# Fetching the rows of every block in quarters of 64 columns and turning them on VectorE

## The chip, the cores and the metric

The kernel runs on one core of a Trainium2 chip. The metric is the device time of one execution in microseconds, as the median of several runs. Where the profile is read, "the span" is the time from the first to the last instruction of one profiled execution.

## The reference: a Fourier mixing, then a mixture of experts

```python
# x: (8, 2496, 256) float32
X = np.fft.fft(x, axis=1)
X = np.fft.fft(X, axis=2)
x = X.real.astype(np.float32).reshape(19968, 256)
logits = x @ w_gate                                # 8 experts
expert_idx = np.argmax(logits, axis=1)
probs = np.exp(logits - logits.max(-1, keepdims=True))
probs /= probs.sum(-1, keepdims=True) + 1e-09
gate_w = probs[np.arange(N), expert_idx]
...
for e in range(E):                                 # rows sorted by expert
    h = np.maximum(x_sorted[lo:hi] @ w1[e], 0.0)   # 256 -> 1024
    y_sorted[lo:hi] = h @ w2[e]                    # 1024 -> 256
return gate_w[:, None] * y_sorted[inv_perm]
```

Each of 19968 rows goes to the one of eight experts that the gate chooses. All data are float32.

## The kernel before

**Two kinds of work are woven into each other.** For each of eight batches the Fourier part (`first`, `regroup`, `second`) computes the batch's 2496 rows, chooses an expert for each (`route`) and scatters the rows, each with its row number and its gate weight behind it (258 floats), to a table `Xs` in DRAM, in which each expert has its own region. The scatter is a series of indirect DMAs on GpSimd's queue (`send`). After a batch, VectorE works out how many full blocks of rows of one expert there are (`plan`), and the expert part (`experts`) works through such blocks. The two parts are generators, and the emission order of the program, which is also each engine's order, follows from how the main loop steps them.

**Blocks.** `rounds` fixes the list of blocks ahead of time: after batch 0 two blocks of 256 rows and four of 128, after batch 1 four of 256, after batch 2 three of 512, after each later batch five of 512, and at the end seven of 256 and 21 of 128 rows, of which a count made at run time says how many are real (`needed`: TensorE branches around the products of the others). These are 66 blocks. `halved(b, size)` is true for the blocks of 512 rows after batch 3 and later and for the seven of 256 rows at the end, 32 blocks; it is false for the other 34 (25 of 128 rows, six of 256, three of 512). Halved blocks compute their first product with seven half-size products in place of eight (`seven`, which needs sums of parts of w1, made by `Left`, and of the rows, made by `right`); the blocks for which `quartered` is true do so with the second product too (`lower`).

**A block's steps.** `fetch_rows` (SyncE's queue) reads the block's rows from `Xs` into one of three buffers `xb`; `fetch_weights` (SyncE's queue, after it) reads w1 and w2 of its expert, 1 MB each, into one of three buffers each. Both are called up to two blocks ahead, and a buffer is free when the block three before is done with it; with `xb` that is its last use of the gate weights, the scaling of `y` on ScalarE (L849 or L674). `turn` brings the rows to the form that the first product needs, columns on the partitions: `xT`[p, c, r] is column 2p + c of row r, with the odd columns' sign changed. There is one buffer `xT`, so a block's turn comes after the first products of the block before. Then TensorE computes `ph` = w1 times `xT` (L222), VectorE (L808) and ScalarE (L810) bring it through the ReLU to `hT`, TensorE computes `py` = `hT` times w2, ScalarE scales it to `y` by the gate weight in `meta` (L849), and GpSimd scatters `y` to the output by the row numbers `ro` (L237; `ro` is made from `meta` at L767). The turn of block k + 1 is stepped between the products `py` of block k, or, where block k is quartered, inside `lower` behind its first, third and fifth product.

**The two ways to turn.** Where `halved` is true, `fetch_rows` reads the rows in four DMAs, one for each quarter of 64 columns (L538): quarter q goes to partitions 32q to 32q + 31, so that row 32j + k of the block lies on partition 32q + k at position j. A fifth DMA (L542) reads the row numbers and gate weights, 8 bytes of each row. VectorE's transpose of 32x32 pieces (L587) then makes `xT` for 256 rows at once, and ScalarE changes the odd columns' sign in place (L589). Where `halved` is false, one DMA (L533) reads whole rows, n = size / 128 neighbouring rows to a partition. TensorE transposes each 128x128 piece, even columns and odd columns, with an identity matrix (L595) to the PSUM tile `pt`, and VectorE multiplies it by +1 and -1 (`alt`) on its way to `xT` (L596).

A DMA on SyncE's queue waits in order, both for its buffer and for the transfer that last used its semaphore.

Of the kernel before, what the change touches and what calls it, by code (L numbers as in the profile page):

```python
# [12 lines left out]
F32 = mybir.dt.float32  # L13
BF16 = mybir.dt.bfloat16
I32 = mybir.dt.int32
ALU = mybir.AluOpType
ACTF = mybir.ActivationFunctionType
# [3 lines left out]
B, S, D = 8, 2496, 256  # L21
# [16 lines left out]
BIG, BLK, REST = 512, 256, 128  # L38
# [8 lines left out]
def free(ap, offset, *dims):  # L47
    return bass.AP(ap.tensor, ap.offset + offset, [list(ap.ap[0])] + [list(d) for d in dims])


def bc(ap, axis, n):
    shape = list(ap.shape)
    shape.insert(axis, n)
    return ap[tuple([slice(None)] * axis + [None])].to_broadcast(shape)


def shape_consts():

    c = {}
    n1 = np.arange(NA)[:, None]  # L60
    r = np.arange(NP)
    k1 = r // 2
    im = r % 2

    def wave(n2, f):
        return f(2 * np.pi / S * ((NB * n1 + n2) * k1 % S))

    w1 = [np.where(im, wave(n2, np.sin), wave(n2, np.cos)) for n2 in range(1, NS)]
    for f in (np.cos, np.sin):
        w1 += [np.where(im, 0.0, wave(0, f)), np.where(im, wave(NS, f), 0.0)]  # L70
    c["w1"] = np.stack(w1, 1) * (k1 < NK)

    u, cs, s = np.meshgrid(np.arange(NU), np.arange(2), np.arange(NS), indexing="ij")
    u, cs, s = (v.reshape(-1, 1) for v in (u, cs, s))
    k2 = np.arange(NB)
    t = 2 * np.pi / NB * ((s + 1) * k2 % NB)
    end = np.where(cs, 1.0 - 2.0 * (k2 % 2), 1.0)
    even = np.where(s == NS - 1, end, np.where(cs, -np.sin(t), np.cos(t)))
    odd = np.where(s == NS - 1, end, np.where(cs, np.cos(t), np.sin(t)))
    own = (u == np.arange(NU)).astype(float)  # L80
    c["m2"] = np.stack([(own[:, :, None] * m[:, None, :]).reshape(GP, GP) for m in (even, odd)], 1)

    rot = np.zeros((GP, GP))
    for p in range(GP):
        if p % NS == NS - 1:
            rot[p, p] = 1.0
        elif p // NS % 2:
            rot[p, p - NS] = -1.0
        else:
            rot[p, p + NS] = 1.0  # L90
    c["rot"] = rot

    d = np.arange(H)[:, None]
    m = np.arange(D + 1)
    t = 2 * np.pi / D * (d * m % D)
    rc, rs = np.cos(t), -np.sin(t)
    rs[0] = 1.0 - 2.0 * (m % 2)
    full = np.concatenate([rc[:, :D], rs[:, :D]], 0)


    rd = np.zeros((H, 2, 2 * E + NY + 1))
    sign = 1.0 - 2.0 * (m[:NY] % 2)
    rd[:, 0, 0:NY] = sign * rc[:, 0:NY]
    rs[0] = 0.0
    rd[0, 1, 2 * E] = 1.0
    rd[:, 1, 2 * E + 1:] = sign * rs[:, 0:NY]
    c["rd"] = rd
    c["alt"] = np.broadcast_to(np.array([1.0, -1.0]), (128, 2))
    c["rt"] = full.T.reshape(2, 128, D).transpose(1, 0, 2)

    p = np.arange(128)[:, None, None, None]
    h = np.arange(2)[None, :, None, None]
    g = np.arange(HW)[None, None, :, None]
    mir = np.arange(2)
    tau = 128 * (HW * h + g) + p
    k1 = tau // NB
    k = k1 + NA * (tau % NB)
    bad = (k1 >= NK) | ((mir == 1) & ((k1 == 0) | (k1 == NK - 1)))
    row = np.where(bad, 0, np.where(mir, S - k, k))
    c["row"] = row.reshape(128, 2, NSL)  # L120
    c["good"] = 1.0 - bad.reshape(128, 2, NSL)
    c["far"] = OUT * bad.reshape(128, 2, NSL)
    c["rev"] = np.broadcast_to(E - np.arange(E), (128, E))
    c["cap"] = np.broadcast_to(CAP * np.arange(E), (128, E))
    c["sgn"] = np.where(np.arange(128) == 0, 1.0, -1.0)[:, None]
    c["lane"] = np.arange(128)[:, None]
    c["tri"] = np.triu(np.ones((128, 128)), 1)
    c["ident"] = np.eye(128)
    return {n: np.ascontiguousarray(v, dtype=np.float32) for n, v in c.items()}


# [60 lines left out]
def halved(b, size):  # L192

    return size == 512 and b > 2 or size == 256 and b == B - 1
# [22 lines left out]
def kernel(ctx: ExitStack, tc, x, w_gate, w1, w2, out):  # L217
    nc = tc.nc
    vec, act, pool = nc.vector, nc.scalar, nc.gpsimd
# [5 lines left out]
    Xs = nc.dram_tensor("Xs", (ROWS, W), F32, kind="Internal").ap()  # L225

    def const_dram(name, v):
        return nc.inline_tensor(v, name=f"c_{name}").ap()
# [17 lines left out]
    def taken(ins, b):  # L246
        ins = getattr(ins, "ins", ins)
        if b + 1 < B:
            tc.declare_no_dep(ins, group=f"xs{b + 1}", reason="a block has rows of its round's batches alone")
        tc.add_to_no_dep_group("taken", ins)  # L250
# [7 lines left out]
    pse = ctx.enter_context(tc.tile_pool(name="pse", bufs=1, space=PSUM))  # L258
# [4 lines left out]

    ctx.enter_context(tc.manual_schedule())
    consts = shape_consts()

    side = [n for n in consts if n not in ("w1", "rt")]
    packed = np.zeros((128, sum(consts[n][0].size for n in side)), np.float32)
    table = cp.tile(list(packed.shape), F32, name="table")
    con, k = {}, 0  # L270
# [9 lines left out]
    wg = cp.tile([128, 2, E], F32, name="wg")  # L280
    tri = cp.tile([128, 128], BF16, name="tri16")
    ones = cp.tile([128, 128], BF16, name="ones16")
    ident = con["ident"]
    waves = const_dram("w1", consts["w1"])

    def load(b, q):
# [239 lines left out]
    def fetch_rows(b, size, tab, i):  # L526


        n = size // 128
        row = nc.sync.value_load(tab[:, 0, i:i + 1], min_val=0, max_val=ROWS - size)  # L530
        xb = bp.tile([128, BIG // 128, W], F32, tag="xb", name="xb", bufs=3)
        if not halved(b, size):
            taken(nc.sync.dma_start(out=xb[:, 0:n].rearrange("p t c -> p (t c)"),  # L533
                                    in_=Xs[ds(row, size)].rearrange("(p t) c -> p (t c)", t=n)), b)
            return xb, xb[:, 0:n, D:]
        flat = xb[:].rearrange("p t c -> p (t c)")
        for q in range(4):
            taken(nc.sync.dma_start(  # L538
                out=flat[32 * q:32 * q + 32, 0:2 * size].rearrange("p (j e) -> p j e", e=64),
                in_=Xs[ds(row, size), 64 * q:64 * q + 64].rearrange("(j k) e -> k j e", k=32)), b)  # L540
        meta = flat[:, 4 * D:4 * D + 2 * n].rearrange("p (t c) -> p t c", c=2)
        taken(nc.sync.dma_start(out=meta, in_=Xs[ds(row, size), D:].rearrange("(t p) c -> p t c", p=128)), b)  # L542
        return flat, meta
# [27 lines left out]
    def right(xs, b11, b12, b21, b22, eng=vec):  # L571

        o = [xs[:, k] for k in range(3)]
        eng.tensor_tensor(o[0], b12, b11, op=sub)
        eng.tensor_tensor(o[1], b22, o[0], op=sub)
        eng.tensor_tensor(o[2], b21, o[1], op=sub)
        eng.tensor_tensor(b12, b22, b12, op=sub)
        return b11, b21, b22, o[2], o[0], o[1], b12

    def turn(b, size, xb):  # L580


        xT = bp.tile([128, 2, BIG], F32, tag="xT", name="xT", bufs=1)
        n = min(size // 128, 2)
        for h in range(-(-size // 256)):
            if halved(b, size):
                vec.transpose(free(xT[:], 256 * h, [32, 8], [BIG, 2], [1, 32]),  # L587
                              free(xb, 512 * h, [64, 8], [1, 2], [2, 32]))
                act.activation(xT[:, 1, 256 * h:256 * h + 256], xT[:, 1, 256 * h:256 * h + 256], ACTF.Copy, scale=-1.0)  # L589
                yield xT  # L590
                continue
            pt = pse.tile([128, 2, n, 128], F32, tag="e", name="pt")
            for c in range(2):
                for t in range(n):
                    nc.tensor.transpose(pt[:, c, t], xb[:, 2 * h + t, c:D:2], ident[:])  # L595
            vec.tensor_tensor(xT[:, :, 256 * h:256 * h + 128 * n], pt[:].rearrange("p c t k -> p c (t k)"),  # L596
                              bc(con["alt"][:], 2, 128 * n), op=ALU.mult)
            yield xT
        if halved(b, size):
            th = size // 2  # L600
            xs = bp.tile([128, 3, th], F32, tag="xs", name="xs", bufs=1)
            r = right(xs, *(xT[:, c, k * th:(k + 1) * th] for c in range(2) for k in range(2)))
            yield r
# [109 lines left out]
    def experts(todo):  # L713
# [35 lines left out]
        for k, (b, size, last, at) in enumerate(todo):  # L749
            n, m = size // 128, BIG // size  # L750
            if not k:
                while todo[0][:3] not in tabs:
                    yield 0, False
                fetch_some(0, 1)
                while b not in whole:
                    yield 0, True
                fetch_some(0)
                for _ in range(9):
                    yield 0, False
                for xT in turn(b, size, xbs[0][0]):  # L760
                    pass
# [163 lines left out]
    for _ in first(0):  # L925
# [8 lines left out]
        out=Xs[E * CAP:].rearrange("(k p) w -> p k w", k=BLK // 128), in_=bc(pad[:], 1, BLK // 128)), "xs"), 0)  # L934
# [100 lines left out]
```

## Time and profile before

| | |
|---|---|
| median of 3 runs | 1286.0 us (1285.17 to 1287.41) |
| the profiled execution's own time | 1297.33 us |
| its span | 1295.5 us |
| mean granted TensorE clock | 0.971 |
| DMA packets of the span | 134023, 249.75 MB, mean 193 GB/s; 85065 of them under 512 B |
| row fetches: whole rows (L533), quarters (L538), their 8-byte parts (L542) | 34, 128, 32 DMAs |

The stages of the span, by the windows view: the time of each stretch, TensorE's matmul and weight-load time, and the share of the 16 DMA engines.

| stretch, us | what runs | PE busy | PEld busy | DMA share | GB/s |
|---|---|---|---|---|---|
| 80 to 142 | rounds 0, batch 1 | 49.2 of 62 | 42.5 | 0.83 | 290 |
| 142 to 245 | rounds 0 and 1, batch 2 | 97.1 of 103 | 86.0 | 0.71 | 245 |
| 245 to 340 | round 2, batch 3 | 94.9 of 95 | 66.5 | 0.49 | 167 |
| 1070 to 1283 | blocks of 256 and 128 rows | 213.0 of 213 | 205.2 | 0.75 | 277 |
| 1283 to 1296 | the last blocks, not real, and the drain | 4.1 of 13 | 1.3 | 0.62 | 228 |

In the profile PE is a matmul on TensorE and PEld the loading of its weights, DVE is VectorE, ACT ScalarE, POOL GpSimd, and SPq the queue of SyncE, which issues most DMAs. A line of a timeline gives the start and the length in us, engine, source line, operation, the tile written and the tiles read, the shapes and a count; in brackets stands how long the engine had been idle and what ended that. "issue" means that it waited for nothing that the profile shows, "remote" and "another core or an unknown queue" that the profile can't name the releaser. L222 is the line of the helper through which all products go, so these are told apart by their tiles.

### The profile page before, as it was taken

Reading aid. Unit: us, or ns where it says so; the run is one execution under the profiler, and the core shown is the slowest. Engines: PE = TensorE matmul, PEld = TensorE weight load, DVE = VectorE, ACT = ScalarE, POOL = GpSimd, SP = SyncE. Lnnn points to the kernel's source line nnn. Section 1 sums busy time; section 2 is a strip of 40 time slices with the busy share of each in tenths; the row PEclk is TensorE's granted clock in tenths of the full one; section 3 lists DMA queues with packets and bytes.
Section 4 is the critical chain, followed back from the end, with each engine's and each line's share of the span. In section 5 each row is a group of like instructions: output and inputs, shape, how many; then the busy total and the mean of one; then the engine's idle time right before and its main releaser. Section 6 shows DMA issues by size and latency. Waiting matters only on the chain.

```text
span 1295.5 us, 20735 instructions
## 1 busy us (share of the span) xinstructions
PE 1237.7 (96%) x7003; PEld 1090.5 (84%) x7003; DVE 700.5 (54%) x1772; ACT 423.4 (33%) x1059; POOL 360.6 (28%) x355
## 2 busy tenths in 40 slices
PE   6769899899999999999999999999999999999997
PEld 4658788687688888888888888888889999999996
DVE  4554145244256655566356655467488774444662
ACT  1423133132244333443234333343333332222222
POOL 0244304314411531135111531145364221111112
PEclk6869999999999999999999999999999999999998
DMA  8877857726636853456433744344355237777776
GB/s 240 275 237 270 310 205 254 276 84 201 201 114 176 277 152 110 141 150 242 120 102 127 241 128 149 98 135 146 107 151 164 90 113 288 276 265 273 290 294 241
DMA packets 134023, 249.75 MB, mean 193 GB/s; under 512 B 85065, under 2 KB 99891, under 8 KB 114332
## 3 DMA queue, kind: packets, MB, share of 16 engines
q1 hardware_dynamic: 117143, 203.33, 48.3%
q0 software_dynamic: 15888, 42.14, 9.0%
q10 hardware_dynamic: 885, 2.94, 0.7%
q8 instruction: 57, 0.93, 0.3%
q14 instruction: 50, 0.41, 0.1%
HBM read 194.97 MB, written 54.83 MB: 193 GB/s over the span
## 4 chain that ended last, share of the span: by engine, by line
PE 70%; issue 18%; DMA 4%; POOL 3%; DVE 2%; another core or an unknown queue 2%; ACT 1%; SPq 0%; POOLq 0%; ACTq 0%; DVEq 0%
PE py L222 28%; PE a L222 7%; PE c L222 7%; PE ph L222 6%; PE p L222 5%; PE d L222 4%; PE b L222 4%; PE s L222 3%; PE e L222 3%; POOL out_dram L237 3%; DMA xq<-in_x_dram 2%; PE pt L595 1%; DMA Xs<-rows,pi 1%; DMA xb<-Xs 0%
## 5 line engine op out<-in xcount | busy, mean ns | idle before, releaser
L222 PE MATMUL py<-w_sb,hT 128*128 128x256 f32 x2016 | 455.9, 381 | 6.5 <-DVE hT L808 3.9
L222 PEld LDWEIGHTS py<-w_sb,hT 128*128 128x128 f32 x2016 | 379.5, 191 | 57.2 <-DVE hT L808 4.3
L237 POOL DMA_INDIRECT out_dram<-y,ro x163 | 160.8, 986 | 729.2 <-ACT y L849 497.9
L237 POOL DMA_INDIRECT Xs<-rows,pi x160 | 163.3, 1020 | 198.3 <-ACT pi L469 103.6
L222 PE MATMUL ph<-xT,w_sb 128*128 128x128 f32 (+2 forms) x992 | 172.4, 329 | 8.5 <-DVE hT L808 6.7
L222 PEld LDWEIGHTS ph<-xT,w_sb 128*128 128x128 f32 x992 | 136.1, 193 | 34.1 <-issue 17.2
L849 ACT ACTIVATE y<-py,xb 128x256 f32<-128x256 f32 x129 | 61.0, 473 | 313.5 <-PE py L222 271.6
L222 PE MATMUL a<-xT,w_sb 128*128 128x256 f32 (+1 forms) x512 | 117.5, 356 | 0.0
L808 DVE TENSOR_SCALAR hT<-ph 128x512 f32<-128x512 f32 x43 | 29.7, 691 | 161.9 <-issue 79.7
L633 DVE TENSOR_TENSOR u<-p,b 128x512 f32<-128x512 f32 x57 | 39.2, 687 | 132.9 <-PE b L222 96.7
L222 PEld LDWEIGHTS a<-xT,w_sb 128*128 128x128 f32 x512 | 89.2, 190 | 10.3 <-issue 0.2
L643 ACT ACTIVATE hT<-a 128x512 f32<-128x512 f32 x57 | 34.0, 597 | 151.2 <-PE a L222 133.6
L410 DVE COPY lg<-p 128x16 f32<-128x16 f32 x80 | 13.9, 174 | 121.0 <-ACT zs L407 117.5
L222 PE MATMUL s<-xq,w 104*112 104x256 f32 (+2 forms) x208 | 62.9, 427 | 11.1 <-DVE xq L299 10.9
L810 ACT ACTIVATE hT<-ph 128x512 f32<-128x512 f32 x55 | 32.8, 597 | 98.2 <-PE ph L222 71.0
L222 PEld LDWEIGHTS p<-table,t 120*128 120x128 f32 x352 | 54.3, 204 | 12.3 <-issue 6.6
L222 PE MATMUL p<-table,t 120*128 120x120 f32 (+1 forms) x352 | 58.2, 290 | 3.8 <-issue 2.7
L222 PE MATMUL c<-xT,ws 128*128 128x256 f32 (+1 forms) x256 | 59.1, 358 | 2.3 <-issue 1.7
L222 PE MATMUL p<-table,zz 128*128 128x145 f32 (+1 forms) x320 | 56.8, 302 | 3.8 <-issue 2.0
L222 PE MATMUL d<-xT,w_sb 128*128 128x256 f32 (+1 forms) x256 | 58.8, 357 | 0.0
L222 PE MATMUL e<-xs,w_sb 128*128 128x256 f32 (+1 forms) x256 | 58.7, 356 | 0.0
L222 PE MATMUL b<-xs,ws 128*128 128x256 f32 (+1 forms) x256 | 58.7, 356 | 0.0
(148 smaller groups left out, 1739.1 us busy)
## 6 DMA issues: line engine op xcount, KB each, us to landing
w_sb<-in_moe_w_dram SPq DMA_DIRECT2D x132, 1024.0 KB
xq<-in_x_dram SPq DMA_DIRECT2D x24, 896.0 KB
xb<-Xs SPq DMA_DIRECT2D x100, 128.0 KB
Td<-t SPq DMA_DIRECT2D x18, 448.0 KB
t<-Td SPq DMA_DIRECT2D x8, 768.0 KB
t<-Td SPq DMA_DIRECT2D x8, 640.0 KB
xb<-Xs SPq DMA_DIRECT2D x25, 129.0 KB
Td<-t ACTq DMA_DIRECT2D x6, 448.0 KB
```

Of the source, the lines that this page charges most:

```text
L222: nc.tensor.matmul(o, lhsT=lhsT, rhs=rhs, start=start, stop=stop, **kw)
L237: return unordered(pool.indirect_dma_start(out=dst, out_offset=bass.IndirectOffsetOnAxis(ap=idx, axis=0), in_=rows, in_offset=None, bounds ...
L410: vec.tensor_copy(lg[:, k:k + 2], p3[:, NY:NY + 2 * E].rearrange("p (m e) -> p m e", m=2))
L595: nc.tensor.transpose(pt[:, c, t], xb[:, 2 * h + t, c:D:2], ident[:])
L633: vec.tensor_tensor(u2[:], p1[:], b[:], op=add)
L643: act.activation(h11, a[:], ACTF.Relu)
L808: vec.tensor_scalar(o, ph[:], 0.0, None, op0=ALU.max)
L810: act.activation(o, ph[:], ACTF.Relu)
L849: act.activation(y[:], py[:], ACTF.Copy, scale=meta[:, i, 1:2])
```

## The change

The branch for whole rows goes out of `fetch_rows`, and the branch with TensorE's transposes out of `turn`. All 66 blocks are fetched in quarters and turned by VectorE, blocks of 128 rows in one piece of 128. The constants `alt` and `ident` go out of the table of constants. `halved` still decides how the products are computed.

```diff
@@ shape_consts
-    c["alt"] = np.broadcast_to(np.array([1.0, -1.0]), (128, 2))
...
-    c["ident"] = np.eye(128)
@@ fetch_rows
         xb = bp.tile([128, BIG // 128, W], F32, tag="xb", name="xb", bufs=3)
-        if not halved(b, size):
-            taken(nc.sync.dma_start(out=xb[:, 0:n].rearrange("p t c -> p (t c)"),
-                                    in_=Xs[ds(row, size)].rearrange("(p t) c -> p (t c)", t=n)), b)
-            return xb, xb[:, 0:n, D:]
         flat = xb[:].rearrange("p t c -> p (t c)")
         for q in range(4):
@@ turn
-        n = min(size // 128, 2)
+        n = min(size, 256)
         for h in range(-(-size // 256)):
-            if halved(b, size):
-                vec.transpose(free(xT[:], 256 * h, [32, 8], [BIG, 2], [1, 32]),
-                              free(xb, 512 * h, [64, 8], [1, 2], [2, 32]))
-                act.activation(xT[:, 1, 256 * h:256 * h + 256], xT[:, 1, 256 * h:256 * h + 256], ACTF.Copy, scale=-1.0)
-                yield xT
-                continue
-            pt = pse.tile([128, 2, n, 128], F32, tag="e", name="pt")
-            for c in range(2):
-                for t in range(n):
-                    nc.tensor.transpose(pt[:, c, t], xb[:, 2 * h + t, c:D:2], ident[:])
-            vec.tensor_tensor(xT[:, :, 256 * h:256 * h + 128 * n], pt[:].rearrange("p c t k -> p c (t k)"),
-                              bc(con["alt"][:], 2, 128 * n), op=ALU.mult)
+            vec.transpose(free(xT[:], 256 * h, [32, n // 32], [BIG, 2], [1, 32]),
+                          free(xb, 512 * h, [64, n // 32], [1, 2], [2, 32]))
+            odd = xT[:, 1, 256 * h:256 * h + n]
+            act.activation(odd, odd, ACTF.Copy, scale=-1.0)
             yield xT
```

More of the change, by code (lines that the diff above doesn't have):

```diff
@@ L282 @@
     ones = cp.tile([128, 128], BF16, name="ones16")
-    ident = con["ident"]
     waves = const_dram("w1", consts["w1"])
```

## The prediction, made before the changed kernel was run

> **What bounds the kernel now.** I read the page's busy shares first, then the slices, then the waits of the touched tiles, then the timeline of each stage that the change touches.
>
> ```profile
> PE 1237.7 (96%) x7003; PEld 1090.5 (84%) x7003; DVE 700.5 (54%) x1772; ACT 423.4 (33%) x1059; POOL 360.6 (28%) x355
> ...
> DMA  8877857726636853456433744344355237777776
> ```
>
> TensorE is busy 96% of the span and carries the chain of waits (the page gives it 70%, and most of the 18% "issue" is time between its own instructions). Each slice is 32.4 us. The DMA row is high at both ends, and there the touched blocks run: the 13 blocks of rounds 0 to 2 (83 to 340 us, slices 3 to 11) and the 21 last blocks of 128 rows (from 1070 us). The 25 blocks of 512 rows between them, and seven of 256 in the last stage, already work in the new way. The answers for the tiles `pt` and `xT` show what the change takes away and what takes its place:
>
> ```profile
> L595 PE MATMUL pt<-table,xb x98: 273/282/488, 86.0 to 1287.9; 128*128 128x128 f32 x98
> L596 DVE TENSOR_TENSOR xT<-pt,table x37: 405/418/692, 87.2 to 1288.4; 128x256 f32<-128x256 f32 x25, 128x512 f32<-128x512 f32 x12
> ```
>
> ```profile
> L587 DVE STREAM_TRANSPOSE xT<-xb x57: 668/704/711, 346.0 to 1253.4; 128x512 f32<-128x512 f32 x57
> L589 ACT ACTIVATE xT<-xT x57: 407/417/419, 346.8 to 1254.2; 128x256 f32<-128x256 f32 x57
> ```
>
> The numbers are ns, shortest/median/longest. In the touched blocks are 98 transposes on TensorE and 37 copies out of PSUM; the lines of L587 and L589 are the turn and the sign change that will take their place.
>
> **Removed: 98 transposes.** Their duration is not their price, because records of TensorE overlap. The timeline of one 128-row block, in the last stage:
>
> ```profile
> 1149.03 0.40 PE L595 MATMUL pt<-table,xb 128*128 128x128 f32 x2
> ...
> 1149.23 0.69 DVE L808 TENSOR_SCALAR hT<-ph 128x512 f32<-128x512 f32 x1 [3.22 <-PE ph L222]
> 1149.26 3.62 PE L222 MATMUL py<-w_sb,hT 128*128 128x256 f32 x16
> 1149.84 0.41 DVE L596 TENSOR_TENSOR xT<-pt,table 128x256 f32<-128x256 f32 x1
> ...
> 1152.50 0.19 PEld L222 LDWEIGHTS ph<-xT,w_sb 128*128 128x128 f32 x1
> ```
>
> From the first transpose's start to the next product's start is 1149.26 - 1149.03 = 0.23 us for two, so 0.115 us each. At 163.68 to 164.15 it is 0.47 for four. The Trainium skill ("TensorE: Matmul & The Clock Gate", Part 4) gives about 275 ns for a transpose in a kernel's context. The record's 282 ns agrees, but it is a latency: by that figure the change would free 98 x 0.275 = 27 us, by the spacing 98 x 0.115 = 11.3 us. I take the spacing. It is the most that can be gained from TensorE's own time.
>
> What of it counts:
> - The 21 last blocks: TensorE is busy 213.0 of 213 us from 1070 to 1283 us, so it is worth its full price there. Of the 42 transposes the last 6 are in the drain after 1283 us, where TensorE mostly waits: 36 x 0.115 = 4.1 us.
> - Rounds 0 to 2: 56 transposes. The first 4 stand behind a wait (below). The next 10 (to 142 us) run ahead of a TensorE stall that ends at 142.2 us (3.9 us for VectorE's hT, then "remote"), while the DMA engines are full; a stall that ends with a transfer swallows what was gained before it: 0. The next 18 (145 to 233 us, 2.1 us) run ahead of a like stall, 3.8 us at 239.9; I count half, 1.0. The last 24 (2.8 us) meet full TensorE until 340 us, but the round after begins with a wait for scattered rows at 336 to 341 us, which the last 8 feed: 16 x 0.115 = 1.8.
> Sum of gains: 4.1 + 1.0 + 1.8 = 6.9 us.
>
> **Added on VectorE and ScalarE.** A turn of 256 rows takes 0.70 us on VectorE where the copy took 0.68 to 0.69. For 128 rows no row stands there: below, half of it, 0.35; above, the whole, 0.70. VectorE's other operations go from 0.69 (512 wide) to 0.42 (256 wide), so I take 0.42, as now. The sign change is new on ScalarE: 12 x 0.42 + 25 x 0.28 (the 128x128 copies of L681 take 0.25) = 12 us in all, on an engine that is 33% busy. What hides both is the second half of the block: in the lines above VectorE finishes hT at 1149.92, would turn until 1150.34 and ScalarE negate until about 1150.65; TensorE needs xT at 1152.50 - 0.23. That is 1.6 us of margin; without it each block would lose the excess. A 128-row block after a 256-row one is turned inside `lower`: there the negation comes after the copy of `p1` in ScalarE's order, so the product that waits for this copy is not held. 0 us.
>
> **Moved: the wait for the rows.** Now TensorE itself waits for xb; then VectorE will, and behind it ScalarE's negation and the y copies. Where rows are early that is nothing. Where they are late, it is the first block of all, on the chain:
>
> ```profile
> 83.36 1.47 SPq L533 DMA_DIRECT2D xb<-Xs  x2
> ...
> 85.99 1.13 PE L595 MATMUL pt<-table,xb 128*128 128x128 f32 x4 [4.50 <-DMA xb<-Xs]
> ...
> 87.90 3.39 PE L222 MATMUL ph<-xT,w_sb 128*128 128x256 f32 x8 [0.78 <-DVE xT L596]
> ```
>
> and the nearest row for what replaces it, the first two fetches of the round at 340 us:
>
> ```profile
> 340.79 1.99 SPq L538 DMA_DIRECT2D xb<-Xs  x4
> 343.29 0.40 SPq L542 DMA_DIRECT2D xb<-Xs  x1
> ...
> 345.98 1.30 DVE L587 STREAM_TRANSPOSE xT<-xb 128x512 f32<-128x512 f32 x2 [5.84 <-DMA xb<-Xs]
> ```
>
> One transfer and a transpose took 87.90 - 83.36 = 4.54 us to the first product. A fetch of 512 rows in quarters took 345.98 - 340.79 = 5.19 us to VectorE's start. For 256 rows the packet records of the fetch at 1242.25 end 3.55 us after its first issue; with the semaphore I take 4.3, then 0.70 turn, and the odd half 0.47 later. First product at 88.4 and the second at 88.85: **+1.0 us**, and the 4 transposes there save nothing. The next start of a round, at 238.80, has 12 us until its xT is needed (251.2): 0. In the drain the last fetch (1283.56) lands about as late as now, but TensorE no longer waits for it (2.8 us at 1287.65): 0 to -0.5, taken as 0.
>
> **Added: 136 DMA issues on SyncE.** 34 fetches become 170 transfers. SyncE spends 343.69 - 340.79 = 2.9 us on a quartered fetch, 0.34 on a whole one. Behind it in SyncE's order stand the next block's w1 and w2, so these start 2.2 to 2.5 us later; in rounds 0 to 2 stores of Td and loads of x also stand there. In the last stage a 128-row block's weights are requested at 1147.86 and used at 1159.8, and 2 MB take 5.5 us: 4 us remain. The tight request is another: w1 of a 256-row block, for which VectorE waits (28.8 us over 6 waits at L569), after which the turned rows are ready 0.8 to 2.0 us before TensorE asks. That fetch is in quarters already, so SyncE doesn't delay it, and the saved transposes take only 0.23 us from the margin: 0.
>
> **Added: small packets.** The Trainium skill ("DMA: Bandwidth & Descriptors", Specifications; also "Rules for kernel authors") speaks against this: transfers under 512 B don't reach line rate. The trace's packet records say how much: 256 B take 21 ns, 8 B 10 ns, 1032 B 58 ns, on one of 16 engines. A 128-row block goes from 128 x 58 = 7.4 to 512 x 21 + 128 x 10 = 12.1 engine-us, +0.3 us. Read as half rate, the rule would make 132 KB at the stage's 277 GB/s 0.5 us longer. If DMA bounded the last stage, 21 blocks would lose 6 us by the trace and 10 by the rule, more than the gain; but its share there is 0.75 and becomes about 0.78, so I take 0. Between 122 and 142 us the engines are full, and two or three fetches there move the end of that stall: about +0.6 us at 0.2 to 0.3 each; bounds 0 and 2.
>
> **Sum** in the profiled execution: -6.9 + 1.0 + 0.6 = -5.3 us; with the drain's half and the +-1 of the stalls I say -6. Span 1295.5 becomes 1289.5, its own time 1297.3 becomes 1291.3. The profiled execution is 11.3 us over the median 1286.0; the difference carries over: **1280 us**.
>
> **The rivals.**
> 1. *All of it counts*: the stalls at 142 and 240 us are not tied to transfers, and shift or shrink. Gain 10 to 11.3, and up to 4.7 more (0.9 + 3.8) if the stall at 240 goes: about 1273. For it: the stalls are put down to "remote" and "issue", not to a DMA. Against: both end as the DMA engines drain. Chance 0.13.
> 2. *Nothing*: rounds 0 to 2 lose 3 to 4 us (longer fetches, full DMA) against 4.1 in the last stage: 1286. For it: DMA share 0.83 from 80 to 142 us. Chance 0.17.
> 3. *Slower*: late weights. Each small fetch holds SyncE 2.2 us longer ahead of w1 and w2, and the small packets lengthen what is in flight. If the DMA engines have no slack in rounds 0 and 1, the 8 blocks fetched from 88 to 191 us pay up to 2.2 us each, 17.6 at most; I take 9. If in the last stage w1 of the 256-row blocks comes late by over about 1 us (its margin), 6 blocks pay the rest, about 0.8 us each, 5 us. Together 14 against the gain of 6.9: 1293. It decides from the point where a fetch plus weights take longer than the block before them (7.2 us). For it: both stages are the DMA's fullest. Against: the order of the tight request, above, and 0.75 share. Chance 0.25.
> That the rows aren't turned rightly is none: the new layout puts row 128t+p at partition p in meta and in xT alike.
>
> **Numbers.** My forecast has 0.45, with a range of its own of 1276 to 1284. No change is within 0.2%, 2.6 us. Faster: 0.45 less its upper edge, and rival 1: 0.57; same 0.17; slower 0.26. Leaving out a tenth at each end: 1272 to 1293.
>
> **What would show it.** Right: no `pt`; 7.0 us instead of 7.25 from one 128-row block's first product to the next; first product of the first block near 88.8; the L569 waits near 29 us. Wrong: TensorE idle after 1070 us behind xT or w_sb; waits before 250 us that grew; SyncE's issues (over 1 us each) ahead of w_sb; stalls at 142 and 240 us moved by several us, which the sum can't foresee.

## The result, and the profile after

The changed kernel takes **1277.5 us** (median of 6 runs, 1275.2 to 1280.6) against 1286.8 (1285.2 to 1287.9, 6 runs beside it): a ratio of 0.9929, 95% interval 0.9913 to 0.9944, or 9.3 us less. The forecast was 1280.

The profiled execution of after has a span of 1273.3 us and its own time is 1275.2. That is 22 us less than before's profiled execution, and more than twice what the medians differ by: before's execution was itself 10.5 us above this median. Which part of these 22 us belongs to the change is the main question below. The page of after, rows as before:

```profile
PE 1220.9 (96%) x6905; PEld 1076.5 (85%) x6905; DVE 700.5 (55%) x1772; ACT 434.8 (34%) x1096; POOL 359.7 (28%) x355
...
DMA  8859988736745743584532843344453238778787
...
DMA packets 163210, 249.71 MB, mean 196 GB/s; under 512 B 118601, under 2 KB 130227, under 8 KB 143516
```

The 98 transposes are gone (7003 matmuls became 6905), VectorE's total has not moved (700.5 before and after), ScalarE has 11.4 us more, and there are 29,000 more packets (33,500 more under 512 B, and fewer of the larger ones that whole rows made). In the last stage (slices 33 to 39 of the DMA row) the engines are busier by a little, 0.80 from 1049 to 1240 us against 0.75 before (1070 to 1283 us). The answer for the tile `xT` gives the new turn, and the timeline the first block (start, length, then as before):

```profile
L579 DVE STREAM_TRANSPOSE xT<-xb x94: 433/699/712, 86.9 to 1267.0; 128x512 f32<-128x512 f32 x69, 128x256 f32<-128x256 f32 x25
L582 ACT ACTIVATE xT<-xT x94: 309/416/418, 87.7 to 1267.6; 128x256 f32<-128x256 f32 x69, 128x128 f32<-128x128 f32 x25
```

```profile
83.00 1.92 SPq L531 DMA_DIRECT2D xb<-Xs  x4
...
86.93 0.71 DVE L579 STREAM_TRANSPOSE xT<-xb 128x512 f32<-128x512 f32 x1 [7.27 <-DMA xb<-Xs]
...
87.70 3.50 PE L220 MATMUL ph<-xT,w_sb 128*128 128x256 f32 x8 [9.12 <-DVE ro L752]
```

The shortest turn, of 128 rows, is 0.43 us (0.42 was taken), the shortest negation 0.31 (0.28). The first product starts 4.70 us after its fetch was issued, against 4.54 before and 5.0 in the prediction.

To see where time came from, I set the last write of chosen blocks against each other in each trace. The 66 blocks are numbered from 0. Stretch A ends with block 11, the second block of 512 rows; C is the last stage, blocks 38 to 62, without its last three blocks; D are those three. Ratios are to the kernel before on the same chip. The pair `before` and `after` is the one of the result above; the four rows from `before_again` to `after_dummy` ran on a chip on which before took 1302.0 us, the four from `after_again` to `early_dummy` on one with 1287.0, the last four on one with 1285.2. One of the twelve runs of `tail_only`, of 1623.4 us at a granted clock of 0.742, is left out of its ratio.

| kernel | ratio (95%) | profiled, own us | A | C | D |
|---|---|---|---|---|---|
| before | 1 | 1297.3 | 328.8 | 216.8 | 6.9 |
| after | 0.9929 (0.9913 to 0.9944) | 1275.2 | 309.6 | 214.4 | 9.6 |
| before_again | one run, 1310.0 us | 1310.0 | 339.4 | 217.0 | 5.9 |
| early_only | 0.9962 (0.9940 to 0.9984) | 1297.3 | 328.7 | 217.1 | 7.4 |
| tail_only | 1.0011 (0.9994 to 1.0029) | 1304.2 | 334.3 | 214.2 | 9.3 |
| after_dummy | 1.0024 (1.0005 to 1.0043) | 1299.2 | 326.3 | 218.7 | 9.2 |
| after_again | 0.9927 (0.9907 to 0.9948) | 1279.7 | 312.4 | 215.8 | 9.4 |
| hybrid | 0.9912 (0.9891 to 0.9933) | 1276.3 | 309.3 | 216.4 | 6.9 |
| weights_first | 0.9910 (0.9890 to 0.9930) | 1272.4 | 306.9 | 212.0 | 11.9 |
| early_dummy | 0.9946 (0.9927 to 0.9965) | 1278.4 | 312.3 | 216.0 | 6.0 |
| early_only_2 | 0.9934 (0.9915 to 0.9953) | 1275.3 | 308.8 | 216.7 | 6.5 |
| early_dummy_2 | 0.9958 (0.9942 to 0.9974) | 1281.0 | 313.5 | 216.0 | 8.2 |
| issues_only | 1.0033 (1.0018 to 1.0047) | 1288.1 | 318.6 | 217.0 | 8.4 |
| best | 0.9895 (0.9877 to 0.9912) | 1272.9 | 311.2 | 212.2 | 5.6 |

Two stretches are left out: the one between A and C, which lies between 736.2 and 740.7 us in all of them, and the one from the last write's start to the end of the span, 3.5 to 5.9 us. Each row is one execution, and executions of one kernel can differ by several us in A (`before` and `before_again`, by 10.6, though on different chips), so the ratios decide and the stretches only say where to look. Already here the picture differs from the prediction's. The last stage, which was to bring most of the gain, is 1.0 to 2.4 us shorter in two traces of the same changed kernel and gives 2.5 to 2.7 us back in D; the gain is in A. Of the 19.2 us between before and after in A, 10.2 lie between before and `issues_only`, whose early rounds are the same.

### The profile page after: what moved, and what is told of

It reads as the page before. It is cut to its first block, busy times and chain, and to the rows that moved or that the text cites. A ratio compares the mean times of both kernels' runs of the same rounds, so it can differ in the third digit from the quotient of the medians.

```text
span 1273.3 us, 21052 instructions
## 1 busy us (share of the span) xinstructions
PE 1220.9 (96%) x6905; PEld 1076.5 (85%) x6905; DVE 700.5 (55%) x1772; ACT 434.8 (34%) x1096; POOL 359.7 (28%) x355
## 2 busy tenths in 40 slices
DMA packets 163210, 249.71 MB, mean 196 GB/s; under 512 B 118601, under 2 KB 130227, under 8 KB 143516
## 4 chain that ended last, share of the span: by engine, by line
PE 86%; DVE 5%; DMA 5%; issue 2%; ACT 1%; SPq 1%; POOL 0%; POOLq 0%; DVEq 0%; ACTq 0%
PE py L220 33%; PE ph L220 11%; PE c L220 10%; PE a L220 9%; PE d L220 6%; PE p L220 6%; PE b L220 5%; PE e L220 4%; PE s L220 3%; DMA w_sb<-in_moe_w_dram 2%; DMA xq<-in_x_dram 1%; DMA Td<-t 1%; SPq L531 0%; DMA xb<-Xs 0%; DVE xq L305 0%
## 5 line engine op out<-in xcount | busy, mean ns | idle before, releaser
L582 ACT ACTIVATE xT<-xT 128x256 f32<-128x256 f32 (+1 forms) x94 | 36.4, 387 | 155.2 <-DVE xT L579 93.1
L579 DVE STREAM_TRANSPOSE xT<-xb 128x512 f32<-128x512 f32 (+1 forms) x94 | 58.3, 628 | 23.5 <-DMA xb<-Xs 23.5
```

What stands on the lines that cost most here:

```text
L579: vec.transpose(free(xT[:], 256 * h, [32, n // 32], [BIG, 2], [1, 32]), free(xb, 512 * h, [64, n // 32], [1, 2], [2, 32]))
L582: act.activation(odd, odd, ACTF.Copy, scale=-1.0)
```

## The experiments

### Which half gains?

`early_only` is the changed kernel with the old fetch and turn kept for the last stage; `tail_only` keeps them for rounds 0 to 2. The other blocks were in quarters before and stay so in both.

```diff
+def inquarters(b, size):
+    return halved(b, size) or b < B - 1          # early_only; tail_only: b == B - 1
...
-        if not halved(b, size):
+        if not inquarters(b, size):
             taken(nc.sync.dma_start(out=xb[:, 0:n].rearrange("p t c -> p (t c)"),
```

> Quarters and VectorE for the 13 blocks of rounds 0 to 2 alone; the 21 last blocks of 128 rows as before. By the prediction's sum: -2.8 + 1.0 + 0.6, so about -1 us, ratio 0.999. By the rival that the early blocks count in full: 52 x 0.115 = 6 us less, ratio 0.995. If a wait of TensorE for rows goes as well: 8 us or more less, ratio 0.994 or lower.

> Quarters and VectorE for the 21 last blocks of 128 rows alone; rounds 0 to 2 as before. By the prediction's sum: -4.1 us, ratio 0.997. By what the changed kernel's trace suggests (each 256-row block longer by up to 0.8 us, the drain longer by about 2.7 us): about -1 us, ratio 0.999.

Measured: 0.9962 (1296.2 us) and 1.0011 (1303.9 us; its interval holds 1). A second run of the first on another chip gave 0.9934, 8.6 us less than before. So **the early rounds bring the whole gain that can be measured, and the last stage none**, the other way round from the prediction's sum (4.1 us from the last stage, 1.2 net from the early rounds).

The kernel before was profiled once more, on the chip of these two runs, to see whether its stalls belong to it:

> The kernel before, unchanged, for a second profile. The first profiled execution took 1297.3 us, 11 us above the median. If the two TensorE stalls at 142 us (3.9) and 240 us (3.8) belong to every execution, they are here again at about the same places and lengths. If they are chance, this execution is some 10 us shorter and the stalls are gone or elsewhere; then the 22 us between the two spans first shown must not be read as the gain.

Its trace has the same pattern, each shifted by some us: TensorE idle for 1.92 us at 124.5, 1.32 at 141.0, 3.89 at 144.3, and 5.0 at 246.8 for rows (`pt<-xb`). This looked like proof that the stall near 140 is a part of the kernel. It is a part of what happens on this chip: `tail_only` and `early_only`, whose profiled executions lie near their medians, have it too (3.89 us at 141.6 and 3.90 at 140.6), and so has `after_dummy` (6.28 at 138.6), whether the early rounds are fetched in the old way or the new. A later run showed that elsewhere the old early rounds can do without it.

### TensorE's time, or its place in the queue?

`after_dummy` is the changed kernel with the 98 transposes put back on TensorE in their old places, on the identity matrix: nothing reads them, and they wait for no transfer.

```diff
         for h in range(-(-size // 256)):
+            if not halved(b, size):
+                pt = pse.tile([128, 2, n // 128, 128], F32, tag="e", name="pt")
+                for c in range(2):
+                    for t in range(n // 128):
+                        nc.tensor.transpose(pt[:, c, t], ident[:], ident[:])
             vec.transpose(free(xT[:], 256 * h, [32, n // 32], [BIG, 2], [1, 32]),
```

> The changed kernel, with 98 transposes on TensorE in the old places, of the identity matrix in place of the rows, so that they wait for no transfer; what they write is read by nobody. If the gain is TensorE's own time, they take back 98 x 0.115 = 11.3 us where TensorE is full, so that the time is back at 1286 or above (ratio about 1.000 or more). If the gain is that TensorE no longer waits for rows in its order, most of it stays: ratio 0.994 to 0.996.

Measured 1.0024. Against the changed kernel's 0.9929 (on another chip, so only roughly comparable) the 98 transposes cost 0.95% or 12 us; 98 x 0.115 is 11.3. The spacing, not the record's 0.28 us (98 of them would be 27 us), is the right price.

`early_dummy` puts only the 56 of the early rounds back, into `early_only`.

> early_only with 56 transposes of the identity matrix on TensorE in the old places of rounds 0 to 2, which wait for no transfer. If the gain there is TensorE's own time, all of it goes (1.000). If it is that TensorE no longer waits in its order for rows and for PSUM, most of it stays (0.996 to 0.997).

Measured 0.9946: about 7 us below before, although TensorE does all its old work again. To size this, both were run on one chip:

> Quarters in rounds 0 to 2 alone, on the same chip as its twin with 56 transposes put back on TensorE. Theory (the gain of the early rounds is TensorE stalls that vanish because TensorE no longer waits in its own order for rows): within 1.5 us of the twin, ratio 0.993 to 0.996. Rival (it is the 56 transposes' own time, 56 x 0.115 = 6.4 us): 4 to 6 us below the twin, 0.989 to 0.991.

> As the one before it, with 56 transposes of the identity put back on TensorE in the old places of rounds 0 to 2: they wait for no transfer and nothing reads them. Theory (stalls that vanish): 0.994 to 0.996, no more than 1.5 us above the kernel without them, and TensorE's idle time from 80 to 345 us near 10 us. Rival (TensorE's own time): 0.998 to 1.000.

Measured: 0.9934 without and 0.9958 with the transposes, medians 1276.6 and 1280.8. The difference is 3.1 us by the ratios (0.0024, and 0 to 6 us by their intervals) and 4.2 us by the medians; A is 4.7 us longer in the one trace than in the other. So neither expectation held alone: **about half of the early gain (the intervals allow none to two thirds) is TensorE's own time; the rest, 5.4 us (3.3 to 7.5, by 0.9958) and 6.9 in `early_dummy`, stays although TensorE does all its old work**. These two kernels keep everything else of the change, the fetch in quarters and VectorE's turn; no run takes away TensorE's wait for rows alone. That it is TensorE's place in the queue is therefore read from the timelines.

It can be seen where round 2 starts with its first block of 512 rows. As the picture of the kernel before I use `issues_only` (below), whose early rounds are those of the kernel before and whose profiled execution lies near before's median. Its timeline:

```profile
219.90 7.07 PE L222 MATMUL ph<-xT,w_sb 128*128 128x256 f32 x32
...
228.78 1.53 SPq L533 DMA_DIRECT2D xb<-Xs  x2
...
232.11 1.13 PE L599 MATMUL pt<-table,xb 128*128 128x128 f32 x4 [5.14 <-DMA xb<-Xs]
233.03 5.82 PE L222 MATMUL py<-w_sb,hT 128*128 128x256 f32 x16
```

and that of after:

```profile
223.99 7.07 PE L220 MATMUL py<-w_sb,hT 128*128 128x256 f32 x32
...
226.83 1.95 SPq L531 DMA_DIRECT2D xb<-Xs  x4
...
231.85 1.31 DVE L579 STREAM_TRANSPOSE xT<-xb 128x512 f32<-128x512 f32 x2 [6.97 <-DMA xb<-Xs]
...
233.26 3.73 PE L220 MATMUL ph<-xT,w_sb 128*128 128x512 f32 x5 [2.20 <-issue]
```

The rows of this block are scattered until just before, so its fetch can't be issued before 227 to 229 us. In the first timeline the transposes that wait for it stand in TensorE's order ahead of the second product of the block before (`py<-w_sb,hT`), so TensorE idles for 5.14 us with 32 matmuls behind the wait, whose operands are there. In the second VectorE waits (6.97 us, at no cost), TensorE does its 32 matmuls meanwhile, and only 2.20 us of idleness remain. The clock adds to it. Two windows views, of `issues_only` and of after (stretch, its length, busy time of PE, PEld, DVE, ACT and POOL, then the granted clock, DMA share, GB/s):

```profile
226.90:232.10 5.20, 0.07 (x1) 0.00 (x0) 0.69 (x1) 0.00 (x0) 0.41 (x1) 0.86 0.49 149
232.10:237.50 5.40, 5.39 (x15) 4.50 (x16) 0.69 (x1) 0.00 (x0) 0.00 (x0) 0.50 0.90 343
```

```profile
231.00:233.30 2.30, 0.10 (x2) 0.07 (x1) 1.36 (x3) 0.65 (x2) 0.00 (x0) 1.00 0.92 181
233.30:237.50 4.20, 4.20 (x6) 1.76 (x7) 0.00 (x0) 1.40 (x4) 1.94 (x2) 0.60 0.89 253
```

After the long idleness the clock was 0.50 for the first 5.40 us of work, a loss of 2.7 us; after the short one 0.60 for 4.20 us, a loss of 1.7. Together with the idleness itself that makes 2.9 + 1.0 = 3.9 us. It is one place in one execution of each kernel, but the size fits what the transposes' time does not explain. `early_dummy_2`, with the same transposes on TensorE but no wait for rows, fits too: at this place TensorE is idle for 0.45 us, no half clock follows, and its A is 5.1 us shorter than that of `issues_only`.

```profile
237.58 8.85 PE L227 MATMUL ph<-xT,w_sb 128*128 128x512 f32 x20 [0.45 <-DVE ro L779]
```

The Trainium skill ("TensorE: Matmul & The Clock Gate", Part 1) has half rate after an idle window of about 3.4 us. The trace has half clock in pieces of 3.4 and 6.8 us, which fits, but a gap of 2.20 us was enough here; by a limit of 3.4 us for the gap the shorter one would have cost nothing beyond itself.

### Why the last stage gains nothing

The prediction's tight spot was w1 of a 256-row block, for which VectorE's L562 (L569 before) waits. In the answer for that line these waits rose from 28.8 to 31.2 us over 6. The first of them in before and in after, from the timelines:

```profile
1088.18 0.36 SPq L548 DMA_DIRECT2D w_sb<-in_moe_w_dram  x1
...
1093.21 0.69 DVE L569 TENSOR_TENSOR ws<-w_sb 128x512 f32<-128x512 f32 x1 [4.17 <-DMA w_sb<-in_moe_w_dram]
```

```profile
1066.21 0.35 SPq L541 DMA_DIRECT2D w_sb<-in_moe_w_dram  x1
...
1072.78 0.69 DVE L562 TENSOR_TENSOR ws<-w_sb 128x512 f32<-128x512 f32 x1 [5.93 <-DMA w_sb<-in_moe_w_dram]
...
1075.32 0.70 DVE L579 STREAM_TRANSPOSE xT<-xb 128x512 f32<-128x512 f32 x1
...
1076.07 1.16 PE L220 MATMUL a<-xT,w_sb 128*128 128x128 f32 x8
...
1082.28 0.94 PE L220 MATMUL c<-xT,ws 128*128 128x128 f32 x6 [0.58 <-DVE hT L624]
```

w1 takes 6.57 us from its issue to its use (5.03 in before), VectorE ends the turn 0.05 us before TensorE starts on it, and VectorE, late with everything else of this block, holds TensorE later on for its hT. From the first product of a 256-row block to that of the next block, six times:

| kernel | us, in order |
|---|---|
| before (last six) | 12.74, 12.74, 12.74, 12.79, 12.93, 12.74 |
| after | 13.53, 12.91, 12.86, 13.15, 12.58, 12.73 |
| after_again | 13.53, 13.22, 13.53, 13.21, 12.58, 12.58 |
| weights_first, best | 12.58, six times |

Without its two transposes such a block would take 12.58; after takes up to 0.95 more. That w1 is slower goes with what was requested just ahead of it, the weights of the block before:

| kernel | w1 requested after the w1 before it by, us | issue to use, us |
|---|---|---|
| before | 8.9, 8.9, 9.6, 10.0, 15.8, 15.1 | 5.03, 5.52, 5.00, 4.88, 4.97, 5.20 |
| after | 7.0, 5.7, 6.0, 6.1, 13.4, 13.6 | 6.57, 6.04, 6.02, 6.28, 4.80, 4.98 |
| issues_only | 7.2, 7.2, 7.2, 8.0, 14.9, 13.2 | 5.23, 5.55, 5.72, 6.21, 4.90, 4.87 |

The fetch of the 256-row block was not delayed (it was in quarters already, as the prediction had it), but the fetch of the 128-row block before it now has five DMAs, so *its* weights start some 2 us later. A row fetch of this stage also waits on SyncE for a weight transfer, 8 times and 7.4 us in all, which before's never do. What this makes on the DMA engines, the windows view shows for the first us after the two requests above: in before the engines are nearly empty then (share 0.17, 18 GB/s), in after they are full (1.09, 241 GB/s). By the packet records it is the weights and, behind them, this block's own rows that end later, so w1 begins later. Where the request before lies 13 us back, w1 is as quick as ever.

`weights_first` turns the order round: in the last stage each block's w1 and w2 are issued ahead of its five row DMAs.

```diff
                 b, size, last, at = todo[k + n]
+                if b == B - 1 and len(got) == n and (b, size, last) in tabs:
+                    got.append(fetch_weights(tabs[b, size, last], at))
                 if (b, size, last) in tabs and b in whole:
                     xbs.append(fetch_rows(b, size, tabs[b, size, last], at))
...
+                if k + len(got) >= len(todo):
+                    continue
```

> The changed kernel, but in the last round SyncE issues a block's w1 and w2 ahead of its five row transfers. If the 256-row blocks got longer because the five issues push the weights back on SyncE's queue, they return to about 12.5 us each (from 12.6 to 13.5) and 1.7 us come back; the drain gets no better, as the last rows now stand behind 2 MB of weights. If the small packets on the DMA engines make them longer, nothing changes there.

Measured 0.9910. C falls to 212.0, 4.8 us below before, all 256-row blocks take 12.58 us, and VectorE no longer waits for w1 at all but for 0.3 us once. The packets are the same and as small (163210 and 118601 under 512 B in both), so **it is the order in which SyncE asks, not the small packets as such, that took the last stage's gain**. D, however, grows to 11.9 us, since now the last rows stand behind 2 MB of weights; the sum of both explains why the total is only slightly below after_again.

`issues_only` asks whether the issues alone do it: the kernel before, with four tiny DMAs (32 rows of 8 bytes, read by nobody) behind each row fetch of a 128-row block of the last stage.

```diff
+            if b == B - 1:
+                tiny = bp.tile([32, 8], F32, tag="tiny", name="tiny", bufs=2)
+                for q in range(4):
+                    nc.sync.dma_start(out=tiny[:, 2 * q:2 * q + 2], in_=x[32 * q:32 * q + 32, 0:2])
             return xb, xb[:, 0:n, D:]
```

> The kernel before, with whole rows and TensorE's transposes, and four tiny transfers (32 rows of 8 B each, which nothing reads) issued on SyncE behind each row fetch of the last stage's 128-row blocks, ahead of the next weights. Theory (SyncE's issues put the weights later, and the weights of the block before then run beside w1 of the 256-row block): about 2 us more on SyncE per fetch, the 256-row blocks grow from 12.74 to about 13.2 us, the stage by 2 to 4 us, ratio 1.001 to 1.003. Rival (small packets of the rows on the DMA engines are what slows the weights): the 256-row blocks stay at 12.74, ratio 1.000.

Measured 1.0033, but not in the way that was expected. The weights do come closer together (7.2 us) and w1 does get slower, by about half as much as in after (table above), but only one of six blocks passes its margin (13.69 us; the rest 12.73 or 12.74), and C is 0.2 us longer instead of 2 to 4. Even that one block says little: `early_only_2`, whose last stage is the old one without tiny DMAs, has 13.45 us at the same place, with w1 6.33 us from issue to use although the weights before it were asked for 9.6 us ahead. So the issues alone do not bring the loss. What after has beyond them, rows in quarters under way just there and a TensorE that is 0.23 us quicker for each block of 128 rows, must have a part in it; no run separates these two. The ratio stands for 4.2 us. C and D together give 1.7 of these; the rest lies in no place that I can name, since no profile of before near its median exists to compare with.

What this run showed by the way is more important. Its early rounds are the kernel before's, and there is no long stall near 140 us. The timeline of before, as profiled:

```profile
131.01 3.73 PE L222 MATMUL ph<-xT,w_sb 128*128 128x128 f32 x32
...
136.31 1.99 PE L222 MATMUL py<-w_sb,hT 128*128 128x256 f32 x8 [1.33 <-issue]
...
141.45 0.69 DVE L808 TENSOR_SCALAR hT<-ph 128x512 f32<-128x512 f32 x1 [13.23 <-remote]
142.20 0.79 PE L222 MATMUL py<-w_sb,hT 128*128 128x256 f32 x1 [3.90 <-DVE hT L808]
```

and the same blocks in `issues_only`:

```profile
128.55 3.73 PE L222 MATMUL ph<-xT,w_sb 128*128 128x128 f32 x32
...
132.35 3.62 PE L222 MATMUL py<-w_sb,hT 128*128 128x256 f32 x16
135.81 3.73 PE L222 MATMUL ph<-xT,w_sb 128*128 128x128 f32 x32
```

The second product takes 3.62 us without a break here; in before it took from 136.31 to about 145.7. A of `issues_only` is 10.2 us shorter than before's, about as much as before's profiled execution lies above its median (10.5). So the stall near 140 is no fixed part of the kernel: of the 14 traces it stands in before's and in all four of the chip with 1302.0 us, and in none of the other nine. It is likely a good part of why that chip is slower, which no run here tests. The prediction counted what "the stall swallows" around it. What makes the stall come and go was not found: in it the DMA engines are full (share 1.05 from 131 to 142 us), but so they are at the same place in `issues_only` (1.04 from 128 to 140), and VectorE waits 13.23 us for a releaser that the trace names "remote", long after the product's records end.

### The end

`hybrid` keeps the old way for the last three blocks of 128 rows only (`b < B - 1 or at < 18` in place of the condition above).

> The changed kernel, but the last three blocks of 128 rows (never real with this input) are fetched as whole rows and turned by TensorE as before. If the drain pays because the last quartered fetch lands behind the weights of the block before it, its 2.4 to 2.7 us come back: 0.002 below after_again, and VectorE's last wait for xb is about 3 us in place of 5. If the drain is set by something else, the two are the same.

Measured 0.9912, which is 0.0015 below `after_again`, beside which it ran; the two intervals overlap widely. D is 6.9 us as before, against 9.4 (to the end of the span, 12.7 against 13.5):

> The changed kernel, unchanged, beside the others of this set. Its first measurement was 0.993 of before. If early_only (0.996) and tail_only (1.001) add up, it is 0.997; if the first measurement holds on every chip, 0.993.

That repeat gave 0.9927, so the result holds on another chip. The ends of before and after show where the 2.7 us in D come from:

```profile
1283.56 0.34 SPq L533 DMA_DIRECT2D xb<-Xs  x1
...
1287.65 0.67 PE L595 MATMUL pt<-table,xb 128*128 128x128 f32 x2 [2.76 <-DMA xb<-Xs]
```

```profile
1259.95 1.96 SPq L531 DMA_DIRECT2D xb<-Xs  x4
...
1262.09 0.36 SPq L535 DMA_DIRECT2D xb<-Xs  x1
...
1267.05 0.45 DVE L579 STREAM_TRANSPOSE xT<-xb 128x256 f32<-128x256 f32 x1 [4.96 <-DMA xb<-Xs]
```

The last fetch is one DMA of 0.34 us before, with 4.09 us from issue to TensorE's start. Now the fifth DMA is issued 2.14 us after the first, and VectorE starts 7.10 us after the first issue. Nothing else is left to do by then, so the 3.0 us show nearly in full at the last write. Not all of it reaches the end of the span, which follows the last write's start by 4.7 us in before and by 3.5 in after: together the end is 1.5 us longer.

### Both repairs together

`best` has the weights first in the last stage, and the old way and order for the last three blocks:

```diff
+                if b == B - 1 and (at < 18 or not last) and len(got) == n and (b, size, last) in tabs:
+                    got.append(fetch_weights(tabs[b, size, last], at))
...
```

> Both repairs together: in the last stage w1 and w2 of a block are requested ahead of its five row transfers, except for the last three blocks of 128 rows, which keep whole rows, TensorE's transposes and rows ahead of weights. Theory (SyncE's order is what loses the last stage's gain, and the last fetch is what lengthens the drain): block 37 to block 62 about 4.5 us shorter than before, as with the weights first alone, every 256-row block 12.6 us long, and block 62 to the end as before (within 0.5 us), so 3 to 5 us below the changed kernel: a ratio of 0.986 to 0.989. Rival (the two repairs act on the same time, since the weights come forward at the cost of rows): no better than either alone, 0.991.

Measured **1272.8 us, 0.9895** (0.9877 to 0.9912) against 1285.2: the quickest of all, some 4 us below the changed kernel by the ratios (0.0032 less than `after_again` on another chip). C is 212.2 and D 5.6, so each repair keeps what it gave alone. Its ratio is a little above the expected 0.986 to 0.989; the interval reaches into it.

```profile
1259.49 0.33 SPq L538 DMA_DIRECT2D xb<-Xs  x1
...
1262.37 0.56 PE L602 MATMUL pt<-table,xb 128*128 128x128 f32 x2 [1.47 <-DMA xb<-Xs]
```

One DMA for the last rows again, and TensorE starts on them 2.88 us after its issue, where VectorE needed 7.10 in after.

## Why the prediction came near the time, and where it failed

The forecast, 1280 us, is 2.5 us above the result and inside its own range (1276 to 1284). **The total is right in good part because two errors of opposite sign cancel.** Its sum had about -4.1 us for the last stage and -1.2 for the early rounds; measured are about +1.4 (`tail_only`, from -0.8 to +3.8 us) and -8.6 (`early_only_2`, from -6.0 to -10.9; -4.9 for `early_only`, on the chip with 1302.0 us).

- **The price of a transpose, 0.115 us: right.** From one 128-row block's first product to the next it takes 7.03 us (1089.60 to 1096.63 in after's timeline), as predicted, and all 98 put back cost about 12 us, though on another chip. The prediction set the record's 282 ns beside the page's 275, which is given for bf16 data; these transposes are float32.
- **The last stage, "36 x 0.115 = 4.1 us": right as a size, but the cover failed.** `weights_first` and `best` show 4.6 to 4.8 us in C once nothing stands in the way.
- **"That fetch is in quarters already, so SyncE doesn't delay it ... 0": the step that failed in the last stage.** The fetch isn't delayed, but the weights ahead of it are, and they then share the DMA engines with it. The step looked at the request that waits and not at what is under way beside it. The term was 0 and measured 2.2 to 3.8 us (C in `after` and `after_again`, 214.4 and 215.8, over C in `weights_first` and `best`, 212.0 and 212.2). Rival 3 had named the mechanism, with 5 us; it was real, but half as large and paid for by the early rounds.
- **The drain, "0 to -0.5, taken as 0": failed.** +2.5 to +2.7 us at the last write, +1.5 at the end of the span (before and after). The prediction took the last fetch to land "about as late as now"; it had the 2.9 us of SyncE's time for a quartered fetch in hand and did not use it here, where nothing hides it.
- **"The next start of a round ... 12 us until its xT is needed: 0", and half of what the stall at 240 swallows: failed, in the other direction.** This is where a good part of the early gain comes from, about 4 us by the two timelines above. The prediction asked when xT is needed *after* the change and found time to spare; it did not ask what TensorE, waiting in order, would do *instead* if it no longer stood there. In three traces of the old early rounds it is a wait for rows of 5.0 to 5.3 us. In before's profile it can't be seen: TensorE's 3.77 us there are a wait for VectorE's hT, which `early_only` has as well (3.72 us at the same product, with VectorE idle for 15.2 us ahead of it in both), so it is a stall of the kind near 140, and the change does not remove it.
- **"A stall that ends with a transfer swallows what was gained before it: 0" at 142 us: failed as a fixed point.** `issues_only`, with the old early rounds, has no such stall. Whether it swallows what was saved ahead of it is not shown; on the chip where every profile has it, `early_only` still gained 4.9 us. Rival 1 (stalls that shift or shrink) was the better description of the early rounds.
- **The first block, +1.0: too dear.** 4.70 us to the first product against 4.54, +0.16 (+0.27 to the end of the first eight products, 3.50 us long against 3.39): the rows were there 3.93 us after the first issue, where 4.3 had been taken, and the first product did not wait for the odd half.
- **VectorE, ScalarE: 0, right.** 0.43 and 0.31 us for the turn and the negation, ScalarE 11.4 us more in all (12 predicted), and both hidden.
- **Small packets: 0, right for the last stage** by `weights_first`, in so far as they cost nothing where the weights go first. Whether they cost the 0.6 us near 130 us can't be told, since executions differ there by more.

Of the signs of being wrong two came: longer waits for w1 in the last stage (31.2 us against 28.8), behind SyncE's issues, and stalls near 142 and 240 us that moved by several us.

## What to carry to other kernels

When a wait moves from one engine to another, count what stands *behind* it on both: here the same late rows cost 5 us while TensorE waited for them in order, and 2 us when VectorE did. When a fetch is cut into more DMAs, its own delay is the smaller part; look at which transfers it pushes into the time of the tightest one. Here it paid to issue the tight ones first, except at the end, where the last rows then stood behind 2 MB. And before a stall is used as a fixed point in a sum, see it in a second execution, near the median and on the same chip: a profile 10.5 us above its median contains 10.5 us that the median does not, and the second profile, from a slower chip, seemed to confirm a stall that the old early rounds can do without elsewhere.

## What was not expected of the hardware

- The same program took 1285.2, 1287.0 and 1302.0 us (medians) on three chips, and the same early rounds (A) took 318.6 to 339.4 us in four profiled executions of them on these chips.
- From 100 us to the drain half clock came in pieces of 3.4 or 6.8 us, and the gap's length alone does not say which: 3.90 us idle (before, at 138) was followed by 3.4 us, 3.17 us (`after_again`, at 232) by 6.8; 1.92 us (`before_again`, at 124) by 3.4, 1.97 us (before, at 120) and 2.08 us (`weights_first`, at 230) by none.
- Five DMAs in place of one take 2.1 to 3.2 us from the first issue to the last in after's last stage, and 1 MB of w1 went from 5.0 to 6.6 us when the weights before it were requested 7 us ahead instead of 9 with the rows of two blocks in quarters around them.
